# A state-space scan with a squared-ReLU FFN behind it: a new order of work for the first three units, and w_in loaded by halves of contraction

## The chip, the cores and the metric

The kernel runs on one core of a Trainium2 chip. The metric is the device time of one execution in microseconds (us). Engines are called by the profile's names: PE multiplies matrices (PEld is its loading of weights), DVE, ACT and POOL work element by element, SP issues DMAs. PSUM, where PE writes, has eight banks of 128 x 512 float32 values.

## The reference, cut to what matters

Per batch (4) and head (8), a sequence of 768 positions is worked through in chunks of 32 with a carried state; the result goes through an FFN with 3072 tokens, 256 columns and 2048 hidden columns.

```python
cum = np.cumsum(la, axis=-1)
L = np.exp(cum[:, :, :, None] - cum[:, :, None, :]) * causal
CB = np.einsum('bhin,bhjn->bhij', Cc, Bc)
y_intra = np.einsum('bhij,bhjd->bhid', CB * L, xc)
y_inter = np.einsum('bhin,bhnd->bhid', Cc, state) * np.exp(cum)[:, :, :, None]
state = decay_full[:, :, None, None] * state + np.sum(Bx, axis=2)
...
h = np.maximum(x @ w_in, 0.0)
return (h * h @ w_out).astype(np.float32)
```

## The kernel before, in words

The work is cut into 12 units of 256 positions of one batch (all heads), three for each batch. Unit k belongs to the batch k mod 4, so units 0 to 3 are the first ones of the four batches and carry no state in. The products of the decays (P) are made once, for the first 256 positions from `a_nat[0]` and for the rest, later, from `a_nat[1]`.

A unit goes through these steps. Its B and C columns are cast or multiplied with P into the tile `jt` (`pb`, `pc`, lines 158 to 170) and transposed on PE (`tr`, line 195; from unit 4 on by a DMA), and the transposed columns are copied out of PSUM into `bct` (`tc`, line 208 on ACT, 210 on DVE). Its x is multiplied with 1/P into `xs` (`px`, line 177). PE makes the scores in four banks (`mt`, line 220); each bank is masked straight out of PSUM on DVE (`mk`, line 229), or copied by ACT (`sc`, 234) and masked from there on POOL or DVE (`ms`, 238). PE sums the new state (`u`) and the output (`in`, in halves `ina` and `inb`; carried state `ca`; all on line 245). The state for the second half of the unit is made from the sums (`sf`, line 343), ACT copies the sums (`us`), and the output is copied into the FFN's input `T` (`t`; on ACT line 208, on DVE 210).

The FFN has 12 blocks, a to l, one for each unit. A lower case token such as a3 is the fourth of eight pairs of hidden columns of block a: four products of 128x256 with w_in on PE (line 403), then ReLU out of PSUM on ACT into `hb` (line 408); the token qa3 squares it on DVE (414); the upper case token A3 is four products with w_out (line 430). So a pair of columns is about 8 matmuls, and the whole FFN is 784 of the kernel's 1623.

The order is written out by hand in the list `ORDER`: each token issues a step (the table in `one`, lines 655 to 704), and the scheduler leaves the order alone, so each engine works through its own tokens strictly in the order of the list. A token's last letter names the engine: v is DVE, a ACT, p POOL, s SP. Banks are given out in turn by `bank` (line 352).

`id` tokens are idle products of ones with ones (line 476) that write to a free bank and are read by nobody; id3:512 is three of 512 columns. `sp`, `su` make the first P and its totals on PE (lines 452, 521), `ps` and `to` copy them out on ACT; `sk` and `sn` are the scans on DVE, `p2` the second P on PE with two copies on ACT behind it, `fq` and `pq` the small products on POOL that turn the totals into `Pquad`; `iv` is the reciprocal of P on DVE (546). `wm` is a small copy that makes ACT load its table.

Loads go over three queues: SP and ACT (`ld` tokens, line 125), and POOL for the weights, which are cast from float32 to bfloat16 on the way (`wi`, line 139, and `wo`, line 143). POOL issues such a transfer between its other work, in the list's order. w_in is four transfers: number i holds pairs 2i and 2i+1, with both halves of the contraction (2 x 128 rows of w_in). w_out is four transfers of two pairs each.

Of the kernel before, what the change touches and what calls it, by code (L numbers as in the profile page):

```python
# [30 lines left out]
def kernel(  # L31
# [26 lines left out]
        sa3 px4 qc1 pc5 pb5 bk c2 rg4 tr5 C0 mk4 mk4 qc2 c7 qc7 sb0 c3 qc3 d2 d1 C5 za4 afC2 d0 C1 px5 C4 qd2 zb3 C6  # L58
        C3 qd0 d3 C2 mk4 mk4 C7 px6 sa4 rg5 qd3 sb3 pc6 zb4 sb4 pb6 D0 d4 qd1 tr6 mk5 za5 zb5 sa5 sb5 D1 iv:64:96 mk5
        d5 qd4 D2 pb7 d6 qd5 d7 qd6 D3 zb2 e0 qd7 mk5 e1 qe0 sb2 D4 mk5 D5 ld8 pc7 e2 qe1 D6 e3 qe2 px7 D7 rg6 e4 qe3  # L60
        za6 sa6 tr7 zb6 mk6 e5 qe4 sb6 e6 qe5 e7 qe6 mk6 E0 E1 E2 E3 ld9 px8 mk6 f0 qe7 E4 f1 qf0 pc8 E5 pb8 E6 mk6
        f2 qf1 f3 qf2 E7 rg7 mk7 F0 f4 qf3 za7 tr8 F1 F2 f5 qf4 f6 qf5 f7 qf6 g0 qf7 zb7 sa7 sb7 mk7 F3 mk7 F4 pc9
        pb9 px9 ld10 g1 qg0 F5 mk7 g2 qg1 F6 g3 qg2 F7 rg8 za8 zb8 sa8 sb8 g4 qg3 G0 mk8 tr9 g5 qg4 G1 mk8 g6 qg5 G2
        g7 qg6 G3 mk8 h0 qg7 G4 pc10 pb10 px10 ld11 h1 qh0 G5 mk8 h2 qh1 G6 h3 qh2 G7 rg9 za9 zb9 sa9 sb9 h4 qh3 H0
        mk9 tr10 h5 qh4 H1 mk9 h6 qh5 H2 h7 qh6 H3 mk9 i0 qh7 H4 pc11 pb11 px11 i1 qi0 H5 mk9 i2 qi1 H6 i3 qi2 H7
        rg10 za10 zb10 sa10 sb10 i4 qi3 I0 mk10 tr11 i5 qi4 I1 mk10 i6 qi5 I2 i7 qi6 I3 mk10 j0 qi7 I4 j1 qj0 I5 mk10
        j2 qj1 I6 j3 qj2 I7 rg11 za11 zb11 sa11 sb11 j4 qj3 J0 mk11 j5 qj4 J1 mk11 j6 qj5 J2 j7 qj6 J3 mk11 k0 qj7 J4
        k1 qk0 J5 mk11 k2 qk1 J6 k3 qk2 J7 rg12 k4 qk3 K0 k5 qk4 K1 k6 qk5 K2 k7 qk6 K3 l0 qk7 K4 l1 ql0 K5 l2 ql1 K6
        l3 ql2 K7 l4 ql3 L0 l5 ql4 L1 l6 ql5 L2 l7 ql6 L3 ql7"""
    WIN = [(0, 2), (2, 4), (4, 6), (6, 8)]  # L70
    WOUT = [(0, 2), (2, 4), (4, 6), (6, 8)]

# [33 lines left out]
    w_in_b = [wpool.tile([128, 2, (f1 - f0) * 256], BF16, name=f"w_in_b{i}") for i, (f0, f1) in enumerate(WIN)]  # L106
# [29 lines left out]
    def load_w_in(i):  # L136
        f0, f1 = WIN[i]
        n = (f1 - f0) * 256
        nc.gpsimd.dma_start(out=w_in_b[i], in_=_dap(moe_w_in, f0 * 256, [[2048, 128], [128 * 2048, 2], [1, n]]))
# [87 lines left out]

    def ph_mask(k, q):
        nc.vector.tensor_tensor(out=live[k]["mts"][:, q].rearrange("p r g i -> p (r g i)"),  # L229
                                in0=pp[:, q, :], in1=mask, op=ALU.mult)  # L230

    def ph_score(k, q):
        sc = big.tile([128, 512], BF16, tag="sc", name=f"sc{k}_{q}")
        nc.scalar.copy(out=sc, in_=pp[:, q, :])
        live[k].setdefault("sc", {})[q] = sc

    def ph_mask_sb(k, q, eng):
        eng.tensor_tensor(out=live[k]["mts"][:, q].rearrange("p r g i -> p (r g i)"),  # L238
                          in0=live[k]["sc"][q], in1=mask, op=ALU.mult)
# [8 lines left out]
    def ph_carry(k, h, begun):  # L248
# [19 lines left out]
    def ph_intra(k, h, begun, qs=range(4)):  # L268
        v = live[k]
        for g in range(2):  # L270
            for r in range(2):
                for i in range(2):
                    for q in qs:
                        hd = 4 * g + q
                        mm(begun, i, [q], pp[32 * q:32 * q + 32, h[i], g * 128:(g + 1) * 128],
                           v["xs"][64 * i:64 * i + 64, r, hd * 32:hd * 32 + 32],
                           v["mts"][64 * i:64 * i + 64, q, r, g, :], (64 * i, 32 * q))

    def ph_t(k, h, engs=None):
# [71 lines left out]

    def bank():
        h = next(h for h in turn if h not in busy)
# [4 lines left out]
    def pair():  # L358
        free = sorted((turn.index(h), h) for h in turn if h not in busy)
# [36 lines left out]
    def mm1(blk, fp):  # L396

        h = bank()
        gi, o = group_of(WIN, fp)
        w = w_in_b[gi]  # L400
        for i in range(2):
            for g in range(2):
                nc.tensor.matmul(pp[:, h, i * 256:(i + 1) * 256],  # L403
                                 _fap(w, g * w.shape[2] + (o // 2) * 512 + 2 * (o % 2) + i, [[4, 128]]),
                                 T[blk][:, g].rearrange("p r u t -> p (r u t)"),
                                 start=(g == 0), stop=(g == 1), skip_group_check=True)
# [49 lines left out]
    with tc.manual_schedule():  # L456
# [131 lines left out]
        def scores(k):  # L588
# [3 lines left out]
            live[k]["todo"] = [0, 1, 2, 3]  # L592
            live[k]["copied"] = []
            live[k]["masked"] = []

        def mask_direct(k):
            q = live[k]["todo"].pop(0)
            ph_mask(k, q)
            busy.discard(q)
            live[k]["masked"].append(q)  # L600

        def score_copy(k):
            q = live[k]["todo"].pop(0)
            ph_score(k, q)
            busy.discard(q)
# [49 lines left out]
        def one(t):  # L655
            f = t.split(":")
            name = f[0].rstrip("0123456789")
            k = int(f[0][len(name):] or 0)
            if len(name) == 1 and name.lower() in "abcdefghijkl" and len(f[0]) == 2:
                blk = "abcdefghijkl".index(name.lower())  # L660
                if name.islower():
                    mm1(blk, k)
# [5 lines left out]
            if name[0] == "q" and len(name) == 2 and name[1] in "abcdefghijkl":  # L668
# [29 lines left out]
                "u": lambda: first_u(k, f[1] if len(f) > 1 else None), "sf": lambda: ph_sd_first(k),  # L698
                "ca": lambda: ph_carry(k, live[k]["h"], live[k]["begun"]),
# [64 lines left out]
```

## Time and profile before

| | us |
|---|---|
| median of 3 runs | 117.8 (117.77 to 117.89) |
| profiled execution | 116.84 |
| its span, from the first to the last instruction | 115.1 |
| start of the first product with w_in (a0) | 12.20 |
| start of the first product with w_out (A0) | 16.96 |

The profile is of one execution. Times in it are counted from the first instruction. A row of a timeline has the start, the length, the engine, the line, the operation, what is written and read, how many instructions were merged, and in brackets the idle time before them with what ended it. A line of a group has busy time, the mean of one in ns, and idle time before it. L430 is line 430 of the kernel before.

### The profile page before, as it was taken

The page shows a single profiled execution, that of the slowest core. Times are in us where ns is not written, and L with a number is a line of the kernel's source. Part 1 is how long each engine was busy: PE and PEld are TensorE (multiplying, and loading weights), DVE is VectorE, ACT ScalarE, POOL GpSimd, SP SyncE. Part 2 cuts the span into 40 slices and gives each one's busy share as a digit, 9 for nine tenths or more (in the row PEclk, how much of TensorE's full clock was granted, in tenths as well). Part 3 has the DMA queues.
Part 4 walks back from the last instruction along what each step waited for, and adds up shares of the span by engine and source line. Part 5 has one row for each costly group of instructions (what it writes and reads, how often), then busy time and mean ns, then how long its engine had stood idle before and what let it go on. Part 6 is the DMA issues. An engine that isn't in the chain of part 4 may idle for free.

```text
span 115.1 us, 3998 instructions
## 1 busy us (share of the span) xinstructions
PE 108.9 (95%) x1623; PEld 93.5 (81%) x1623; DVE 84.2 (73%) x187; ACT 76.7 (67%) x161; POOL 49.8 (43%) x102
## 2 busy tenths in 40 slices
PE   7977969999999999999999999999999999999990
PEld 2344749978898989989989989989989899899980
DVE  2469996779599969969965989849668488445530
ACT  0655667865598756787486686786777776876840
POOL 7369972068599457548602669038020020000000
PEclk9999999999999999999999999999999999999999
DMA  1999999989999913935915926623023020020202
GB/s 29 199 196 145 199 203 189 215 167 210 180 191 211 214 24 108 160 89 155 179 46 122 178 97 123 132 95 73 0 100 68 0 100 0 6 91 0 91 0 91
DMA packets 47814, 13.46 MB, mean 117 GB/s; under 512 B 44276, under 2 KB 45876, under 8 KB 47796
## 3 DMA queue, kind: packets, MB, share of 16 engines
q1 hardware_dynamic: 43828, 10.64, 44.8%
q0 software_dynamic: 1664, 2.10, 10.8%
q10 hardware_dynamic: 2304, 0.48, 2.0%
q8 instruction: 12, 0.20, 0.8%
q14 instruction: 6, 0.05, 0.1%
HBM read 10.58 MB, written 3.15 MB: 119 GB/s over the span
## 4 chain that ended last, share of the span: by engine, by line
PE 87%; DMA 6%; POOL 2%; issue 1%; DVE 1%; ACT 1%; ACTq 0%; DVEq 0%
PE pp L430 36%; PE pp L403 36%; PE pp L245 6%; DMA w_out_b<-in_moe_w_out_dram 6%; PE pp L476 4%; PE pp L220 3%; POOL mts L238 1%; PE pp L195 1%; POOL jt L158 1%; PE pp L452 1%; DVE jt L158 0%; DVE Sd L343 0%; ACT bct L208 0%; PE pp L521 0%; ACT osl L722 0%
## 5 line engine op out<-in xcount | busy, mean ns | idle before, releaser
L408 ACT ACTIVATE hb<-pp 128x512 bf16<-128x512 f32 x96 | 55.0, 599 | 24.7 <-PE pp L403 23.1
L430 PE MATMUL pp<-w_out_b,h 128*128 128x256 bf16 (+1 forms) x400 | 54.3, 268 | 0.8 <-DMA w_out_b<-in_moe_w_out_dram 0.8
L414 DVE TENSOR_TENSOR h<-hb 128x512 bf16<-128x512 bf16 x96 | 45.0, 486 | 12.7 <-ACT hb L408 12.3
L403 PE MATMUL pp<-T,w_in_b 128*128 128x256 bf16 x384 | 54.2, 273 | 0.0
L403 PEld LDWEIGHTS <-w_in_b 128*128 128x128 bf16 x384 | 41.4, 114 | 2.2 <-issue 1.0
L430 PEld LDWEIGHTS <-h 128*128 128x128 bf16 x400 | 37.6, 98 | 5.4 <-DVE T L210 1.1
L229 DVE TENSOR_TENSOR mts<-pp,mask 128x512 bf16<-128x512 f32 x45 | 29.6, 677 | 3.3 <-PE pp L220 3.3
L331 POOL TENSOR_TENSOR Sd<-z,Pquad 128x256 bf16<-128x256 f32 x16 | 11.1, 693 | 32.9 <-DVE z L315 25.7
L177 POOL TENSOR_TENSOR xs<-x_nat,Pinv 128x256 bf16<-128x256 f32 (+1 forms) x19 | 14.4, 776 | 5.2 <-DVE Pinv L546 4.6
L158 POOL TENSOR_TENSOR jt<-C_nat,P_sb 128x128 bf16<-128x128 f32 x22 | 9.4, 449 | 1.5 <-ACT P_sb L688 1.0
L476 PE MATMUL pp<-const-bfloat16-1.0 128*128 128x512 bf16 (+2 forms) x19 | 7.3, 516 | 0.8 <-PEq L748 0.8
L315 DVE SCALAR_TENSOR_TENSOR z<-z,Ptot,us 128x64 f32<-128x64 f32 x8 | 2.2, 281 | 6.3 <-ACT us L299 5.4
L437 ACT COPY osb<-pp 128x512 f32<-128x512 f32 x11 | 6.3, 584 | 0.4 <-PE pp L430 0.4
L245 PE MATMUL pp<-mts,xs 64*32 64x128 bf16 x384 | 5.9, 219 | 0.1
L170 POOL CAST jt<-B_nat 128x128 bf16<-128x128 f32 x17 | 5.4, 341 | 1.4 <-DMA B_nat<-in_B_dram 1.4
L220 PE MATMUL pp<-bct 32*64 32x256 bf16 x192 | 5.1, 279 | 0.9 <-DVE bct L210 0.6
L476 PEld LDWEIGHTS <-const-bfloat16-1.0 128*128 128x128 bf16 x19 | 2.2, 122 | 4.0 <-issue 3.7
L245 PEld LDWEIGHTS <-xs 64*32 64x32 bf16 x384 | 4.2, 90 | 0.6 <-issue 0.4
L282 ACT CAST T<-pp 128x512 bf16<-128x512 f32 x7 | 4.1, 592 | 0.4 <-PE pp L245 0.2
L208 ACT CAST T<-pp 128x256 bf16<-128x256 f32 x8 | 2.6, 375 | 2.6 <-PE pp L245 2.6
L245 PE MATMUL pp<-bct,Sd 128*128 128x128 bf16 x40 | 4.2, 220 | 0.0
L220 PEld LDWEIGHTS <-bct 32*64 32x64 bf16 x192 | 2.1, 102 | 2.0 <-issue 0.6
(62 smaller groups left out, 53.4 us busy)
## 6 DMA issues: line engine op xcount, KB each, us to landing
x_nat<-in_x_dram SPq DMA_DIRECT2D x11, 256.0 KB, 3.7
out_dram<-osb SPq DMA_DIRECT2D x11, 256.0 KB, 3.2
B_nat<-in_B_dram SPq DMA_DIRECT2D x11, 128.0 KB, 3.1
C_nat<-in_C_dram SPq DMA_DIRECT2D x11, 128.0 KB, 3.4
w_in_b<-in_moe_w_in_dram POOLq DMA_DIRECT2D x4, 256.0 KB, 6.8
w_out_b<-in_moe_w_out_dram POOLq DMA_DIRECT2D x4, 256.0 KB, 8.2
x_nat<-in_x_dram ACTq DMA_DIRECT2D x2, 128.0 KB, 3.4
bct<-jt SPq DMA_TRANSPOSE x8, 3.6
```

Source lines behind the costliest of these rows:

```text
L158: eng.tensor_tensor(out=_fap(jt[k % 3], 128 + 144 * g, [[384, 2], [32, 4], [1, 16]]), in0=_fap(loaded[k]["C"], 128 * g, [[16, 2], [32, 4], ...
L177: eng.tensor_tensor(out=_fap(xs, 256 * r, [[256, 2 // n], [32, 8], [1, 32]]), in0=_fap(loaded[k]["x"], 32 * r, [[32, 2 // n], [64, 8], [1, ...
L220: nc.tensor.matmul(pp[64 * u:64 * u + 64, q, r * 256:r * 256 + 256], bct[32 * q:32 * q + 32, r, 0, u * 64:u * 64 + 64], _fap(bct[32 * q:32 ...
L229: nc.vector.tensor_tensor(out=live[k]["mts"][:, q].rearrange("p r g i -> p (r g i)"), in0=pp[:, q, :], in1=mask, op=ALU.mult)
L245: nc.tensor.matmul(dst, w, v, start=bool(need), stop=False, skip_group_check=True, **({} if pos is None else {"tile_position": pos}))
L331: nc.gpsimd.tensor_tensor(out=_fap(S_d, 0, [[128, 2], [32, 4], [1, 32]]), in0=_fap(z, 0, [[32, 2], [0, 4], [1, 32]]), in1=_fap(Pquad, 4 * ...
L403: nc.tensor.matmul(pp[:, h, i * 256:(i + 1) * 256], _fap(w, g * w.shape[2] + (o // 2) * 512 + 2 * (o % 2) + i, [[4, 128]]), T[blk][:, g].r ...
L408: nc.scalar.activation(out=hb.rearrange("p i t -> p (i t)"), in_=pp[:, h, :], func=AF.Relu)
L414: nc.vector.tensor_tensor(out=h2, in0=hb, in1=hb, op=ALU.mult)
L430: nc.tensor.matmul(dst, h2[:, i, r * 128:(r + 1) * 128], w_out_b[gi][:, 2 * o + i, c0:c1], start=first, stop=(fp == 7 and i == 1), skip_gr ...
L437: nc.scalar.copy(out=osb, in_=pp[:, 6 if blk == 1 else 7, :])
L476: nc.tensor.matmul(pp[:, h, 0:int(cols)], ones_b[:, 0:128], ones_b[:, 0:int(cols)] if dep is None else dep, start=True, stop=True, skip_gr ...
```

## The change

The list `ORDER` is new up to the third unit; from `rg4` on it is as before. `WIN` has two groups of four pairs, and the four transfers of w_in are by pair group and half of contraction: transfers 0 and 1 are the two halves for pairs 0 to 3, transfers 2 and 3 for pairs 4 to 7. The destination of each is 1024 adjacent columns instead of two runs of 512. A token such as a3:0 issues only the two products of a unit that read the first half, a3:1 the other two; in between the bank stays taken. `sf` can be made on ACT, in four activations, one for each quarter. There are 24 idle products instead of 19. Further functions (masks by halves, T by halves, banks named in the list) are added and not used: `HALF` is empty, and the list has no `tg` and no `@`.

```diff
-        id3:512 fa1:a la fa0:s ku ef ldx0:h:a eb id2:512 ti id1:512 gB3 pi ldB0:l:a hd ldC0:l:a ldB0:h:s ldC0:h:s
-        ldx0:l:a wm jz0:v mb jz1:v ldB1:s id3:512 sk pbh0:a id2:512 pk pbl0:p wi0 sp pc0:v ldC1:s trB0 wi1 su iv1:0:8
-        trC0 tcC0:0:v tcB0:2:a id1:512 tcC0:1:a ps pb1:a to px0:v jz2:v mt0 id1:512 u0:67 ldx1:s pc1:p fq sc0 mk0
-        id1:512 mk0 ms0:p tr1 tc1:1:v sc0 tc1:0:a sf0 mt1 ldB2:s wo0 ldC2:s ms0:v ldx2:s id1:384 in0 ca0 iv:8:16
-        id3:512 px1:p t0:aa id1:256 mk1 a0 a1 mk1 mk1 mk1 u1 ina1 inb1 sn1 us0 sf1 qa0 a3 ldC3:s wi2 fr p2 wi3 ca1
-        qa1 wo1 pc2 pb2:a t1:vv us1 iv:32:64 a2 zb0 qa2 zb1 A0 ldB3:s wo2 ldx3:s b3 qb3 b0 pq b2 b1 tr2 wo3 sb1 qa3
-        qb0 A1 b5 b4 qb1 qb2 qb5 tc2:1:v qb4 tc2:0:a a5 B0 b6 B1 a7 qa5 iv:16:32 px2 a6 mt2 B3 A2 sc2 u2 b7 us2 pb3:a
-        pc3 mk2 qa6 px3 mk2 A5 ms2:v mk2 ld4 qb6 sf2 a4 qa7 B5 pc4 A6 A3 ld5 pb4 ina2 inb2 tr4 ca2 t2:aa tr3 B4 B2
-        tc3:0:a tc3:1:a u3:45 qb7 ld6 ld7 mt3 qa4 B6 mk3 mk3 mk3 mk3 us3 c4 c5 c0 A4 A7 B7 c6 qc0 za3 qc4 c1 qc5 qc6
+        id3:512 id1:384 ef pi ti id2:512 id2:512 ku la fa1:a eb id2:512 jz0:v jz2:v fa0:s jz1:p ldx0:h:a ldB0:l:a
+        ldB0:h:s mb wm ldC0:l:a ldC0:h:s ldB1:s sk ldx0:l:a hd wi0 sp id3:512 ldC1:s ps iv:8:16 id2:512 pbh0:p
+        iv1:0:8 pc0:v pbl0:p pk trB0 su tcB0:2:a trC0 ldx1:s tcC0:0:a tcC0:1:v px0:v to id1:512 mt0 id1:128 id2:512
+        mk0 wi1 id1:384 pb1:a u0:67 pc1:p sc0 wi2 tr1 fq id1:128 id1:512 sc0 ms0:p sf0:a wo0 tc1:0:a mk0 tc1:1:v
+        ms0:v ldB2:s mt1 px1:p in0 ca0 id1:256 mk1 ldC2:s t0:aa a1 a0 fr mk1 mk1 ldB3:s u1 ldx2:s us0 mk1 ina1 sf1
+        us1 a2 inb1 ca1 wi3 iv:16:32 ldC3:s a3:0 t1:aa qa1 qa0 id1:512 a3:1 b3 wo1 zb1 sn1 b1 b0:0 ldx3:s p2 pq b0:1
+        wo2 qa3 qb1 iv:32:64 A0 pc2 a5 b4 a6 b6 qb0 qa2 b2 b5 pb2:p qa5 tr2 A1 qb4 sb1 qb3 qa6 tc2:0:a A2 a7 qb2
+        px2:v wo3 B0 pc3 B2 B3 qb5 tc2:1:a mt2 ld4 u2 B1 A5 sf2 qa7 sc2 mk2 B5 mk2 pb3:a ms2:v sc2 ca2 a4 A6 b7 ms2:v
+        tr3 px3:p ina2 inb2 pc4:v us2 tc3:1:v qa4 A3 tc3:0:v qb6 B4 t2:aa mt3 mk3 u3:45 pb4:p qb7 B6 mk3 px4:p ld5
+        tr4 us3 mk3 mk3 c4 qc4 c5 c0 pc5:v ld6 A4 pb5:v c6 qc0 B7 A7 za3 sa3 c1 bk zb0 ld7 qc5 c2 qc1 qc6 rg4 tr5 C0
...
-    WIN = [(0, 2), (2, 4), (4, 6), (6, 8)]
+    WIN = [(0, 4), (4, 8)]
...
-    w_in_b = [wpool.tile([128, 2, (f1 - f0) * 256], BF16, name=f"w_in_b{i}") for i, (f0, f1) in enumerate(WIN)]
+    w_in_b = [wpool.tile([128, 1024], BF16, name=f"w_in_b{i}") for i in range(4)]
...
     def load_w_in(i):
-        f0, f1 = WIN[i]
-        n = (f1 - f0) * 256
-        nc.gpsimd.dma_start(out=w_in_b[i], in_=_dap(moe_w_in, f0 * 256, [[2048, 128], [128 * 2048, 2], [1, n]]))
+        h, g = i // 2, i % 2
+        nc.gpsimd.dma_start(out=w_in_b[i], in_=_dap(moe_w_in, h * 1024 + g * 128 * 2048, [[2048, 128], [1, 1024]]))
...
+        if eng is nc.scalar:
+            for q in range(4):
+                nc.scalar.activation(out=_fap(S_d, 32 * q, [[128, 2], [1, 32]]),
+                                     in_=_fap(pp, v["h"][0] * 512 + 256, [[32, 2], [1, 32]]),
+                                     func=AF.Copy, scale=Pquad[:, total(0, b, 0), q:q + 1])
...
-    def mm1(blk, fp):
+    def mm1(blk, fp, part=None):
 
-        h = bank()
+        h = opened.pop((blk, fp)) if part == 1 else bank()
...
-            for g in range(2):
+            for g in (0, 1) if part is None else (part,):
                 nc.tensor.matmul(pp[:, h, i * 256:(i + 1) * 256],
-                                 _fap(w, g * w.shape[2] + (o // 2) * 512 + 2 * (o % 2) + i, [[4, 128]]),
+                                 _fap(w_in_b[2 * gi + g], (o // 2) * 512 + 2 * (o % 2) + i, [[4, 128]]),
```

More of the change, by code (lines that the diff above doesn't have):

```diff
@@ L59 @@
[L59 to L63, printed above, removed]
@@ L350 @@
     busy = set()
+    forced = []
     def bank():
-        h = next(h for h in turn if h not in busy)
+        h = forced.pop(0) if forced else next(h for h in turn if h not in busy)
+        assert h not in busy
         turn.remove(h)
@@ L358, in pair @@
     def pair():
+        if forced:
+            return tuple(bank() for _ in range(2))
         free = sorted((turn.index(h), h) for h in turn if h not in busy)
@@ L591, in scores, with read_out @@
             busy.update(range(4))
-            live[k]["todo"] = [0, 1, 2, 3]
+            live[k]["todo"] = [(g, p) for g in range(2) for p in range(2)] if k in HALF else [0, 1, 2, 3]
             live[k]["copied"] = []
             live[k]["masked"] = []
+        def read_out(k, q):
+            if k not in HALF:
+                busy.discard(q)
+            elif q[0]:
+                busy.difference_update((2 * q[1], 2 * q[1] + 1))
         def mask_direct(k):
@@ L622, in intra @@
             v = live[k]
+            if k in HALF:
+                gs = {"": (0, 1), "a": (0,), "b": (1,)}[part]
+                assert all((g, p) in v["masked"] for g in gs for p in range(2))
+                ph_intra(k, v["h"], v["begun"], range(4), gs)
+                return
             qs = v["masked"][{"": slice(0, 4), "a": slice(0, 2), "b": slice(2, 4)}[part]]
@@ L655, in one @@
         def one(t):
+            t, _, at = t.partition("@")
+            forced[:] = [int(c) for c in at]
             f = t.split(":")
```

81 lines of the change are left out of this document (60 added, 21 removed).

## The prediction

> **What bounds the kernel now.** I read the page's busy line first, then the table by stretches, then the chain of waits, then the timelines of PE, ACT and POOL.
>
> ```profile
> span 115.1 us, 3998 instructions
> PE 108.9 (95%) x1623; PEld 93.5 (81%) x1623; DVE 84.2 (73%) x187; ACT 76.7 (67%) x161; POOL 49.8 (43%) x102
> ```
> ```profile
> 12.20:16.96 4.76, 3.68 (x78) 2.77 (x77) 4.69 (x12) 2.81 (x10) 4.28 (x9) 1.00 1.18 201
> 16.96:30.33 13.37, 13.26 (x206) 11.38 (x207) 9.85 (x24) 9.88 (x24) 5.30 (x9) 1.00 1.10 194
> 30.33:35.77 5.44, 5.44 (x114) 4.88 (x107) 5.11 (x9) 4.25 (x10) 5.30 (x11) 1.00 1.12 187
> 35.77:115.10 79.33, 76.41 (x1120) 69.75 (x1112) 57.11 (x124) 54.24 (x105) 26.56 (x51) 1.00 0.39 90
> ```
> PE bounds the kernel: 95% of the span. In the stretches (columns: length, then busy time of PE, PEld, DVE, ACT, POOL, granted clock, DMA share, GB/s) it is whole from 30.33 on; what 35.77 to 115.10 lacks is the last stores. The two order lists are equal from the token `rg4` on, and PE's first unit behind it (C0) starts at 35.77 in the trace of before. So the change is worth what it does to the moment at which PE reaches C0; after that the same PE work follows, in the same order.
>
> ```profile
> 0.85 4.85 PE L476 MATMUL pp<-const-bfloat16-1.0 128*128 128x512 bf16 x11 [0.85 <-PEq L748]
> 5.63 0.64 PE L452 MATMUL pp<-eye_f,cp 64*64 64x32 f32 x8
> 7.24 0.40 PE L195 MATMUL pp<-eye_b,jt 128*128 128x128 bf16 x4
> 8.09 0.42 PE L220 MATMUL pp<-bct 32*64 32x256 bf16 x16 [0.24 <-ACT bct L208]
> 10.31 0.42 PE L220 MATMUL pp<-bct 32*64 32x256 bf16 x16 [0.64 <-DVE bct L210]
> 10.94 0.45 PE L245 MATMUL pp<-mts,xs 64*32 64x128 bf16 x32
> 11.44 0.93 PE L476 MATMUL pp<-const-bfloat16-1.0 128*128 128x512 bf16 x4
> 12.20 1.03 PE L403 MATMUL pp<-T,w_in_b 128*128 128x256 bf16 x8
> 16.96 0.60 PE L430 MATMUL pp<-w_out_b,h 128*128 128x256 bf16 x4 [0.81 <-DMA w_out_b<-in_moe_w_out_dram]
> 17.39 1.91 PE L403 MATMUL pp<-T,w_in_b 128*128 128x256 bf16 x16
> 30.78 1.47 PE L403 MATMUL pp<-T,w_in_b 128*128 128x256 bf16 x12
> 32.09 1.47 PE L430 MATMUL pp<-w_out_b,h 128*128 128x256 bf16 x12
> ```
> ```profile
> 10.33 6.49 DMA w_out_b<-in_moe_w_out_dram
> ```
> Twelve FFN products start every 1.31 us (30.78 to 32.09), 0.109 each; a unit (four, a lower or upper case token) is 0.44. The FFN starts at 12.20. From there to 16.96 PE is idle for 4.76 - 3.68 = 1.08. A product is drawn 0.27 long while the next starts after 0.11, so at each of four stops 0.16 more is lost: some 1.7 in all. The chain says why it ends at 16.96: A0, the first product with w_out, stands ahead of everything else, and w_out_b0 is on its way for 6.49, from 10.33 to 16.82. From 16.96 to 30.33 only 0.11 of idle and three or four such ends: some 0.55. That is the stock: **2.3 us**, if the FFN did not start later.
>
> **Part 1, from the scan to the first FFN product.** Eleven idle products take 4.85, so 0.43 each; the four at 11.44 run at 0.22 (three of 512 columns and one of 256 in 0.76). In the new list nine and a 384 stand ahead of the token sp: 9 x 0.43 + 0.32, they end at 5.0. sp waits for the scan anyway; I put it at 5.5 (5.63 before). New behind it: five idle products ahead of the B transposes, from about 6.1. Cold they are 2.1 long, at full speed 1.1; the trace is cold at 5.5 and fast at 7.24, and I take one cold and four fast: they end at 7.35. They are partly cover, since DVE now makes two reciprocals ahead of the two C products:
>
> ```profile
> 6.31 0.49 DVE L158 TENSOR_TENSOR jt<-C_nat,pp 128x128 bf16<-128x128 f32 x2 [0.96 <-PE pp L452]
> 7.34 0.26 DVE L546 RECIPROCAL Pinv<-pp 128x16 f32<-128x16 f32 x1 [0.54 <-PE pp L521]
> 3.56 1.28 ACT L487 ACT_TABLE_LOAD   x1 [3.56 <-issue]
> C_nat<-in_C_dram ACTq DMA_DIRECT2D x1, 64.0 KB, 3.2
> ```
> The first (`iv:8:16`) waits for ACT's copy of P (`ps`), which moved ahead of the C products. sp's end at 6.3, the copy 0.2, two reciprocals and two products: the C columns are done at about 7.5 instead of 6.8, and trC0, behind five idle products and su, runs at 7.75 instead of 7.24, the scores of unit 0 (mt0) at 8.5 instead of 8.09. **Loads:** the token `wm` now makes ACT load its table (1.28) ahead of the low halves of C0 and x0; SP's queue keeps its order up to C2, then B3 stands ahead of x2 and C3. C0 is issued at about 3.85 and lands 3.2 later, at 7.0, just when DVE is there; x0 goes 0.5 behind it and is needed at 8.4. I cost both at nothing; each us more would go straight onto the FFN's start.
>
> ```profile
> 5.67 0.30 ACT L512 ACTIVATE pick_p<-pick,cp 64x8 f32<-64x8 f32 x1
> 8.56 1.07 ACT L234 CAST sc<-pp 128x512 bf16<-128x512 f32 x2
> 9.55 0.48 ACT L208 COPY bct<-pp 128x384 bf16<-128x384 bf16 x1
> 11.43 0.65 ACT L208 CAST T<-pp 128x256 bf16<-128x256 f32 x2 [1.41 <-PE pp L245]
> 12.84 1.09 ACT L408 ACTIVATE hb<-pp 128x512 bf16<-128x512 f32 x2 [0.76 <-PE pp L403]
> 15.53 0.17 ACT L538 COPY Ptot<-pp 128x16 f32<-128x16 f32 x1 [0.46 <-PE pp L537]
> 15.59 0.27 ACT L539 COPY P_sb<-pp 128x128 f32<-128x128 f32 x1
> ```
> `sf0:a` makes unit 0's state on ACT in four activations where DVE made one. No row has that shape: below, 0.06 each (Ptot to P_sb, start to start), above, 0.30 (pick_p); I take 0.15, nearer to the copies out of PSUM, so 0.6 (0.24 to 1.2). They stand ahead of tc1:0, the copy (0.48) that unit 1's scores (mt1) wait for; in before it was free on ACT at 9.55. New: two score copies from 8.97 to 10.05, four activations to 10.6, the copy to 11.05, mt1 at 11.1 instead of 10.31. Less of the 384 idle product goes between mt1 and unit 0's sums, so those are at 11.46 instead of 10.94. From there to a0 it was 1.26 (to 12.20), bound by T's two copies; so the first FFN product is at **12.65, 0.45 later** (0.1 to 1.0 by the bounds). The idle products among these are hidden by the same ACT chain.
>
> **Part 2, w_in.** Two transfers by halves of contraction now hold four pairs of columns for both halves, so a0 to a3 and b0 to b3 need w_in_b0 and 1, the rest 2 and 3.
>
> ```profile
> 5.61 1.64 POOL L139 DMA_DIRECT2D w_in_b<-in_moe_w_in_dram  x2 [0.17 <-issue]
> DMA to landing us min/median/max: 5.5/6.8/7.6
> DMA to landing us min/median/max: 6.5/8.2/8.3
> ```
> The landing rows are of w_in, then of w_out. POOL issues the first at about 4.0 (5.61 before) and the second at 5.8, so both are in by 11.3 to 12.3, or 13.4 at the worst: hidden ahead of 12.65, up to 0.75 if not. The third goes at about 8, w_out_b0 at 10.7, w_in_b3 at 12.3. So w_out_b0 lands at 17.2.
>
> **Part 3, from 12.65 to A0.** PE has a1, a0, u1, a2, unit 1's sums, carry and a3 (cut in two, with a 0.22 idle product between) up to 15.4. T1's copies are ACT's now (DVE's before), behind three hb copies of 0.6: done at 15.75, a wait of 0.4. Then b3, b1, b0 and p2: A0 at **17.75**. That is after w_out_b0, so the old wait is gone. Before, A0 was at 16.96 with four units of 0.44 behind it; now seven: 3 x 0.44 - 0.79 = **0.52 ahead**. With the 0.55 of stops behind 16.96, which have to be earned again, up to 1.07.
>
> **Part 4, what is late next: w_out_b2 and 3.**
>
> ```profile
> 14.22 0.78 POOL L158 TENSOR_TENSOR jt<-C_nat,P_sb 128x128 bf16<-128x128 f32 x2
> 15.78 0.40 POOL L542 TENSOR_TENSOR Pquad<-Ptot,quad 128x64 f32<-128x64 f32 x1 [0.24 <-ACT Ptot L538]
> 16.14 0.59 POOL L143 DMA_DIRECT2D w_out_b<-in_moe_w_out_dram  x1
> 18.30 0.61 POOL L331 TENSOR_TENSOR Sd<-z,Pquad 128x256 bf16<-128x256 f32 x1 [1.57 <-DVE z L320]
> 28.12 0.92 POOL L170 CAST jt<-B_nat 128x128 bf16<-128x128 f32 x2
> ```
> On POOL `pq` now stands behind w_out_b1 and ahead of everything of unit 2 and of w_out_b2 and 3. It waits for Ptot, which ACT copies after p2, and p2 has moved behind b0: 17.9 instead of 15.7. POOL stands still from 13.5 to 17.9. Then pq 0.4, w_out_b2 0.6, two products 0.8, two casts 0.9, Sd 0.6: w_out_b3 is issued at 21.3 instead of 16.14. tr2 waits for the casts at 20.7; PE is there at 20.8: no cost, but no cover either. A5, which needs w_out_b2 (18.35 + 6.5 = 24.9), comes at 24.7. A6, the first that needs w_out_b3, stands 17 units (7.43) and 1.0 of small products behind A0: 26.2. The landing is 5.5 to 6.5 after the issue, by the fastest w_in and w_out: 26.8 to 27.8, a stall of 0.6 to 1.6. Below that, queues emptier than in any row could make it nothing; I take 0.8. While PE stands, DVE and ACT catch up with unit 2 and 3, so I add only 0.2 for the other stops.
>
> **The sum:** 0.52 + 0.55 - 0.8 - 0.2 = 0.07 gained. The profiled execution took 116.84 (span 115.1) beside a median of 117.8; the difference of 1.0 lies around the span, so 117.73: **117.7 us**, no change that can be measured. A measurement of this kernel tells about 0.2% (0.24 us) from no change.
>
> Two rules beside the trace. The profile's granted clock reads 1.00 in all stretches, the first too, where products took 0.43: the cadence decides. The Trainium skill, "TensorE: Matmul & The Clock Gate", Part 1, says that the clock opens after a busy window of about 3.4 us that runs free of the kernel's start, so that the number of cold products varies by run; the trace agrees with one change, between 5.5 and 7.24; how far it varies no run here shows. By it a late window would make the five new products cold, the third rival.
>
> ```profile
> q0 software_dynamic: 414, 0.67, 105.4%
> q1 hardware_dynamic: 351, 0.04, 15.0%
> ```
> In the window 18.5 to 22 the weights' queue (q0) and SP's (q1) moved 414 and 351 packets: near one for one, though q0's are far larger. The Trainium skill, "DMA: Bandwidth & Descriptors", section "Queues, rings and completion order", says that each DMA engine goes round the queues that have work, a packet each; the counts agree. By it w_out_b3, alone in its queue, would pass SP's backlog in some 2 us (an estimate) and land without a stall at A6: the sum would be 0.8 better, as in the first rival.
>
> **The rivals.** *w_out in time* (faster): without A6's stall the sum is 0.87, 116.9; for it speaks that q0 holds nothing else then, against it that even the first w_in took 5.5. *w_out late* (slower): the place is A6, the price the landing of w_out_b3 less 26.2; it decides from a landing at 27.1 on, where a stall of 0.9 has eaten the lead. At 27.8 (6.5) the sum is 0.73 the other way, 118.5; if A5 and tr2 are late too, by 0.2 and 0.3, 119.0; I give 118.7. A landing after 8.2, the median of w_out, at 29.5, would be a stall of 3.3 and 120.2, the far end. *Late clock* (slower): the four idle products that I took as fast cost 0.21 more each, 0.85 onto mt0 and all behind it: 118.6. Against it: three runs within 0.12. *The change does nothing*: a0 waits for T, not for w_in, and the lead is spent on stops of the same length: 117.8.
>
> **How the numbers follow.** Forecast 117.7, own range 117.2 to 118.2, chance 0.44 (faster 0.17, within 0.2% 0.19, slower 0.08); w_out in time 0.19, faster; w_out late 0.23, slower; late clock 0.10, slower; nothing 0.04, within. Faster 0.36, same 0.23, slower 0.41. The range 116.8 to 119.0 leaves out the quick end of the first rival and the far end of the second.
>
> **What would show it.** The first w_in product (12.65), mt1 (11.1), T1's copies and A0 (17.75) in the timeline of PE; POOL idle before pq, released by ACT's Ptot; a wait of PE for w_out at A6, and when C0 starts against 35.77. Wrong: a first product past 13.2, or one before 12.2; no wait for w_out behind A0; PE idle for T1 over 1 us; C1 or x0 landing late because the larger w_in packets take their place.

## The result, and the profile after

The changed kernel takes **125.25 us** (median of 4 runs, 124.33 to 126.10) beside 117.78 of the kernel before (4 runs): ratio 1.0648, 95% interval 1.0554 to 1.0743. The forecast was 117.7 with a range up to 119.0. The ratios here and below leave out executions that were over 1.5% longer than the fastest of the same kernel, which the medians do not, and the profiles of e4, e8, e9 and e10 are of such executions.

The page of the profiled execution (125.62 us), first the span and the engines, then the row of the granted clock in 40 slices of 3.1 us:

```profile
span 123.9 us, 4001 instructions
...
PE 112.6 (91%) x1626; PEld 95.0 (77%) x1628; DVE 87.7 (71%) x191; ACT 78.4 (63%) x164; POOL 46.6 (38%) x98
...
PEclk9998559999679999999999999999999999999999
```

The span is 8.8 longer, and the clock row, all 9 before, has two dents: at slices 4 to 6 and at 11 and 12. The table by stretches (length, then busy time of PE, PEld, DVE, ACT, POOL, clock, DMA share, GB/s) cuts the time at unit 0's sums (12.55), just behind the starts of the first FFN product (16.31) and of A0 (22.72), around a stop behind B0 (27.64 to 31.10), and just behind the start of C0 (44.54), from which on both lists are equal:

```profile
9.06:12.55 3.49, 0.55 (x3) 0.19 (x3) 0.97 (x2) 0.93 (x2) 3.18 (x6) 0.84 1.06 187
12.55:16.48 3.93, 3.53 (x77) 1.94 (x77) 3.27 (x7) 1.99 (x7) 2.12 (x3) 0.50 1.06 175
16.48:22.94 6.46, 6.03 (x91) 4.55 (x90) 4.15 (x12) 4.57 (x13) 0.00 (x0) 0.86 0.98 182
...
27.64:31.10 3.46, 0.60 (x6) 0.31 (x4) 3.46 (x4) 1.48 (x4) 2.56 (x5) 1.00 1.08 191
31.10:44.59 13.49, 13.49 (x251) 10.59 (x249) 10.53 (x28) 8.39 (x21) 1.33 (x3) 0.87 0.45 81
44.59:123.90 79.31, 76.35 (x1117) 69.69 (x1112) 57.80 (x125) 54.31 (x105) 27.77 (x54) 1.00 0.41 89
```

The starts are rows of PE's timeline:

```profile
16.31 1.87 PE L441 MATMUL pp<-T,w_in_b 128*128 128x256 bf16 x8 [0.25 <-ACT T L210]
...
22.72 0.60 PE L473 MATMUL pp<-w_out_b,h 128*128 128x256 bf16 x4
...
30.88 1.05 PE L473 MATMUL pp<-w_out_b,h 128*128 128x256 bf16 x8 [2.86 <-DVE h L457]
...
44.54 0.61 PE L473 MATMUL pp<-w_out_b,h 128*128 128x256 bf16 x4
```

From C0 to the end it is 79.36 here and 79.33 before: the whole difference was made ahead of C0, which comes at 44.54 instead of 35.77, 8.77 later. Two stretches have next to no PE work, 9.06 to 12.55 and 27.64 to 31.10, and behind each of them PE works at a lower clock (0.50, then 0.87).

**The first stop.** The chain of waits (start, length, what) has it in one row:

```profile
1.23 3.18 DMA x_nat<-in_x_dram
4.41 0.02 issue
4.43 7.06 DMA x_nat<-in_x_dram
...
11.58 0.92 DVE xs L179
12.50 0.04 issue
12.55 0.33 PE pp L263 x10
```

x0's low half is not issued until x0's high half has landed (1.23 + 3.18 = 4.41): the two transfers share a semaphore. Eight semaphores serve these loads in turn; x0's low half was the ninth load to take one, and is the eleventh in the new list (C1, too, goes ahead of it). Then it takes 7.06, where it took 3.3 before (the last number of the row below; KB, us from issue to landing), and unit 0's sums stand at 12.55 instead of 8.77.

```profile
x_nat<-in_x_dram ACTq DMA_DIRECT2D x1, 128.0 KB, 3.3
```

In the meantime POOL, too, waits 2.65 for C1. What held them up is seen by queue (packets, MB, share of the 16 DMA engines' time; q0 carries the weights, q1 SP's loads, q10 ACT's), first in the stretch 6 to 7 us, then in 7 to 8:

```profile
q1 hardware_dynamic: 610, 0.08, 49.1%
q10 hardware_dynamic: 323, 0.08, 36.0%
q0 software_dynamic: 14, 0.03, 28.1%
```
```profile
q0 software_dynamic: 56, 0.11, 78.7%
q10 hardware_dynamic: 90, 0.02, 11.1%
q1 hardware_dynamic: 5, 0.00, 0.8%
```

POOL issued w_in_b0 at 4.21; its packets begin between 6 and 7. One microsecond later 56 packets of weights hold the engines for 78.7% of the time, SP's queue has gone from 610 packets to 5 and ACT's from 323 to 90.

**The second stop.** The waits up to 35 us (total, times, longest) name DVE's squares, and the wait of pq in POOL's queue (it is put down to the square that ended last; Ptot, which pq reads, was copied by ACT at 22.69, behind p2):

```profile
POOL Pquad L585 <- DVE h L457: 8.3, 1, 8.3
...
PE pp L473 <- DVE h L457: 2.9, 1, 2.9
```

The timelines of DVE, then of POOL, in the same microseconds:

```profile
23.57 7.26 DVE L457 TENSOR_TENSOR h<-hb 128x512 bf16<-128x512 bf16 x7
```
```profile
22.95 0.29 POOL L585 TENSOR_TENSOR Pquad<-Ptot,quad 128x64 f32<-128x64 f32 x1 [8.27 <-DVE h L457]
23.19 0.59 POOL L145 DMA_DIRECT2D w_out_b<-in_moe_w_out_dram  x1
23.80 0.99 POOL L160 TENSOR_TENSOR jt<-C_nat,P_sb 128x128 bf16<-128x128 f32 x2
...
27.36 1.04 POOL L179 TENSOR_TENSOR xs<-x_nat,Pinv 128x512 bf16<-128x512 f32 x1
28.35 0.71 POOL L172 CAST jt<-B_nat 128x128 bf16<-128x128 f32 x2
29.03 1.18 POOL L179 TENSOR_TENSOR xs<-x_nat,Pinv 128x256 bf16<-128x256 f32 x2
```

Seven squares take 7.26, over 1 us each on average and up to 1.98, where before three took 1.14. pq comes through at 22.95, and then POOL does in one unbroken run, up to 30.2, what it had spread from 14 to 30 before.

### The profile page after: what moved, and what is told of

Its sections match the earlier page's. It is cut to its first block, busy times and chain, and to the rows that moved or that the text cites. A ratio compares the mean times of both kernels' runs of the same rounds, so it can differ in the third digit from the quotient of the medians.

```text
span 123.9 us, 4001 instructions
## 1 busy us (share of the span) xinstructions
PE 112.6 (91%) x1626; PEld 95.0 (77%) x1628; DVE 87.7 (71%) x191; ACT 78.4 (63%) x164; POOL 46.6 (38%) x98
## 4 chain that ended last, share of the span: by engine, by line
PE 83%; DMA 8%; DVE 3%; ACT 2%; issue 1%; ACTq 0%; DVEq 0%
PE pp L473 36%; PE pp L441 35%; DMA x_nat<-in_x_dram 8%; PE pp L263 7%; PE pp L222 4%; DVE h L457 2%; ACT Sd L370 1%; DVE xs L179 1%; ACT T L210 1%; PE pp L197 1%; DVE Sd L375 0%; ACTq L118 0%; PE pp L495 0%; ACT bct L210 0%; PE pp L580 0%
## 5 line engine op out<-in xcount | busy, mean ns | idle before, releaser
L473 PE MATMUL pp<-w_out_b,h 128*128 128x256 bf16 (+1 forms) x400 | 55.5, 273 | 2.9 <-DVE h L457 2.9
L457 DVE TENSOR_TENSOR h<-hb 128x512 bf16<-128x512 bf16 x96 | 48.8, 526 | 11.1 <-ACT hb L451 11.0
L441 PE MATMUL pp<-T,w_in_b 128*128 128x256 bf16 x384 | 55.1, 276 | 0.3 <-ACT T L210 0.2
L241 DVE TENSOR_TENSOR mts<-pp,mask 128x512 bf16<-128x512 f32 x44 | 29.0, 679 | 2.3 <-PE pp L222 2.3
L179 POOL TENSOR_TENSOR xs<-x_nat,Pinv 128x256 bf16<-128x256 f32 (+1 forms) x18 | 13.3, 759 | 0.1
L160 POOL TENSOR_TENSOR jt<-C_nat,P_sb 128x128 bf16<-128x128 f32 x18 | 8.0, 462 | 2.7 <-DMA C_nat<-in_C_dram 2.7
L519 PE MATMUL pp<-const-bfloat16-1.0 128*128 128x512 bf16 (+3 forms) x22 | 7.7, 479 | 0.9 <-PEq L811 0.8
L263 PE MATMUL pp<-xs,jt 64*32 64x64 bf16 x160 | 3.1, 206 | 2.9 <-DVE xs L179 2.9
L263 PEld LDWEIGHTS <-jt 64*32 64x32 bf16 x160 | 1.7, 92 | 5.1 <-issue 4.3
```

What stands on the lines that cost most here:

```text
L160: eng.tensor_tensor(out=_fap(jt[k % 3], 128 + 144 * g, [[384, 2], [32, 4], [1, 16]]), in0=_fap(loaded[k]["C"], 128 * g, [[16, 2], [32, 4], ...
L179: eng.tensor_tensor(out=_fap(xs, 256 * r, [[256, 2 // n], [32, 8], [1, 32]]), in0=_fap(loaded[k]["x"], 32 * r, [[32, 2 // n], [64, 8], [1, ...
L263: nc.tensor.matmul(dst, w, v, start=bool(need), stop=False, skip_group_check=True, **({} if pos is None else {"tile_position": pos}))
L441: nc.tensor.matmul(pp[:, h, i * 256:(i + 1) * 256], _fap(w_in_b[2 * gi + g], (o // 2) * 512 + 2 * (o % 2) + i, [[4, 128]]), T[blk][:, g].r ...
L457: nc.vector.tensor_tensor(out=h2, in0=hb, in1=hb, op=ALU.mult)
L473: nc.tensor.matmul(dst, h2[:, i, r * 128:(r + 1) * 128], w_out_b[gi][:, 2 * o + i, c0:c1], start=first, stop=(fp == 7 and i == 1), skip_gr ...
```

## The experiments

Each changed kernel was run beside the kernel before on the same chip. "List" is the order list; moves are shown as its fragments.

| run | what it is | us, median | ratio to before, 95% |
|---|---|---|---|
| after | the change | 125.25 | 1.0648 [1.0554, 1.0743] |
| e1 | C0's and x0's low halves ahead of ACT's table load | 123.90 | 1.0546 [1.0482, 1.0610] |
| e2 | pq back behind w_out_b3 | 122.69 | 1.0442 [1.0383, 1.0501] |
| e3 | e1 and e2 | 121.17 | 1.0345 [1.0252, 1.0439] |
| e4 | before's list, new w_in layout | 118.29 | 1.0065 [1.0026, 1.0103] |
| e5 | w_in issued later | 120.34 | 1.0203 [1.0131, 1.0275] |
| e6 | e5 and e2 | 119.31 | 1.0148 [1.0090, 1.0205] |
| e7 | e6, loads ahead as in e1 | 119.74 | 1.0147 [1.0056, 1.0239] |
| e8 | sixteen idle products in the first stop | 126.08 | (122.82 to 127.92, no interval) |
| e9 | e7, two idle products more ahead of sp | 118.95 | 1.0213 [1.0159, 1.0267] |
| e10 | e9 with the old w_in layout | 117.95 | 1.0086 [1.0037, 1.0136] |
| e11 | e10, three idle products fewer | 117.88 | 1.0125 [1.0067, 1.0184] |
| e12 | before, with three POOL products more | 117.77 | 1.0151 [1.0082, 1.0221] |
| e13 | the change with the old w_in layout | 126.13 | 1.0630 [1.0532, 1.0728] |
| e14 | before, with w_in issued earlier | 119.37 | 1.0130 [1.0070, 1.0189] |

**e1, e2, e3: the two stops, by undoing one move each.** e1 is the change with the loads' fragment altered, e2 with pq's, e3 with both.

```diff
- ldx0:h:a ldB0:l:a ldB0:h:s mb wm ldC0:l:a ldC0:h:s ldB1:s sk ldx0:l:a hd wi0 sp
+ ldx0:h:a ldB0:l:a ldC0:l:a ldB0:h:s ldC0:h:s ldx0:l:a mb wm ldB1:s sk hd wi0 sp
```
```diff
- p2 pq b0:1
+ p2 b0:1
...
- px2:v wo3 B0
+ px2:v wo3 pq B0
```

> One part undone: the low halves of C0 and x0 are issued by ACT ahead of its table load, and B1 behind them, as in the kernel before; the rest is the changed kernel. Theory (two separate stalls: x0's low half late behind w_in, and later squares held up by POOL): x0's low half lands by 7.5 instead of 11.49, unit 0's sums (u0) start at 9.1 to 9.8 instead of 12.55, the first product with w_in comes at 12.3 to 13.2 instead of 16.48, the half clock from 11.4 to 18.3 is gone, and the time is 119.5 to 122; the stall at B2 stays. Rival (the larger w_in packets, issued early, starve whatever is loaded beside them, wherever x0 stands): x0 or the next load (C1, x1) is late all the same, u0 or mt1 still waits over 2 us for a load, and the time is 123.5 to 125.5.

> Only the token pq moves: from ahead of w_out_b2 to behind w_out_b3, so POOL no longer stands still from w_out_b1 to the second P. Theory (squares on DVE are held up while POOL works without a pause behind pq): squares between 23 and 31 take about 0.4 instead of up to 2.0, PE's wait of 2.9 at B2 falls under 0.5, the half clock from 31.9 to 35.3 is gone, and the time is 120 to 122.5; the stall at u0 stays. Rival (the squares wait for hb, or DVE for x2 by a load that is late): the squares stay late, PE waits over 2 at B2, and the time is 124 to 125.5.

> Both edits together. Theory (the two stalls and the clock that they cost are the whole loss): 116.5 to 118.3, with the first product with w_in at 12.3 to 13.2 and no half clock before the end. Rival (starved loads): above 120.

e1 fell to the rival: 123.9. Ahead of ACT's table load x0's low half still stood in front of a taken semaphore (now that of the second transfer of a_nat) and was issued at 4.4. It came 2 us sooner all the same, the sums were at 10.37, and POOL then waited 4.2 for C1. e2 was 122.69, 0.2 past what the theory gave. Its timeline of DVE:

```profile
25.08 2.11 DVE L457 TENSOR_TENSOR h<-hb 128x512 bf16<-128x512 bf16 x5
```

The squares are back at 0.42, the stop behind B0 and the second dent of the clock are gone: pq's place is worth about 2% of this kernel as long as the first stop is there. In e3 (rival again: 121.17) the sums come at 10.42, and the timeline of PE shows the next load in line:

```profile
11.83 0.96 PE L197 MATMUL pp<-eye_b,jt 128*128 128x128 bf16 x5 [0.99 <-POOL jt L160]
```

These are unit 1's transposes behind POOL's product with C1. The first stop is no matter of x0 alone; with x0 mended, C1 is late.

**e4: the layout alone.** The list of before in the changed kernel.

> The other way round: the list of the kernel before, with only w_in loaded by halves of contraction in rows of 1024 columns. Theory (the layout by itself does no harm where w_in goes out after x0): 117.2 to 118.4, x0 and C1 landing as before. Rival (larger w_in packets starve the loads): x1, B2 or C2 land more than 2 us later than in the kernel before, and the time is over 119.

118.29, ratio 1.0065: as the theory had it, a small loss, and no stop ahead of unit 0's sums. In the profiled execution (119.74) PE waits 1.36 and 1.28 for the third and fourth transfers of w_in, at 20.9 and 22.5.

**e5, e6, e7: w_in's first transfer later.** e5 is the change with one move; e6 adds e2's, e7 also issues the loads ahead of the table load, with the first transfer of a_nat ahead of the second.

```diff
- hd wi0 sp
+ hd sp
...
- pc0:v pbl0:p pk
+ pc0:v pbl0:p wi0 pk
```

> The changed list with one move: POOL issues w_in_b0 behind its two B0 copies (about 5.6 instead of 4.21); everything else as changed, pq too. Theory (the early w_in transfer starves the small-packet loads x0 low half and C1, which are issued at 4.4 and 4.0): x0's low half lands by 8.5 instead of 11.49, C1 by 9, PE's stall ahead of unit 0's sums falls from 3.5 us to under 1, the half clock at 11.4 goes, and the stall at B2 behind pq stays: 119.5 to 122. Rival (the loads are late because they are themselves issued late, behind their semaphore slots, and any w_in transfer in flight then does the same): x0 low still lands beyond 10, and the time is 123.5 to 125.5.

> As the run before, and pq stands behind w_out_b3 again. Theory (two separate causes that add): both stalls gone, no half clock after 7 us, 116.8 to 118.5. Rival (a third cause is left: C1, with w_in_b1 issued at about 6.1 to 6.6): POOL still waits for C1 over 2 us, mt1 beyond 13, 119 to 121.5.

> As the run before, and the low halves of C0 and x0 are issued ahead of ACT's table load, with the first a transfer ahead of the second as before the change, so that x0's low half meets a free semaphore slot. x0 low is expected issued at about 3.0 and landed by 6.5. Theory (loads decide the start, the new layout and the idle products cost next to nothing): first FFN product at 12.2 to 12.7, 116.5 to 117.8. Rival (the two-kilobyte packets of w_in still slow C1 and x1 enough to delay mt1 by 1 us or more): 118 to 119.5.

e5's theory held for the loads and for the time. w_in_b0 is issued at 5.79. In the stretch 7 to 8 us, where the changed kernel had 5 packets of SP's queue, it has

```profile
q1 hardware_dynamic: 1057, 0.24, 111.6%
q10 hardware_dynamic: 36, 0.01, 3.8%
```

and none of weights. x0's low half, issued at 4.54 behind the same taken semaphore as in the changed kernel, landed 3.7 later, and the timeline of PE runs through, up to the first products with w_in:

```profile
9.63 0.25 PE L263 MATMUL pp<-xs,jt 64*32 64x64 bf16 x16
...
11.37 0.42 PE L222 MATMUL pp<-bct 32*64 32x256 bf16 x16 [0.77 <-ACT bct L210]
...
14.03 0.95 PE L441 MATMUL pp<-T,w_in_b 128*128 128x256 bf16 x7 [0.85 <-DMA w_in_b<-in_moe_w_in_dram]
```

Unit 1's scores (the second row) are at 11.37; the forecast had 11.1. So 1.6 us of issue time on one transfer is worth 4.5% here (1.0648 to 1.0203), with everything else of the change in place. One part of the theory failed: the stop behind B0 should have stayed, since pq stands where it stood, and it shrank from 2.86 to 0.23:

```profile
25.00 1.05 PE L473 MATMUL pp<-w_out_b,h 128*128 128x256 bf16 x8 [0.23 <-DVE h L457]
```

pq comes through at 19.71 here, and POOL's unbroken run ends at 24.3, where it waits for x2. So the two stops are not separate causes: most of the second one came with the early w_in too.

With pq moved too, e6 and e7 stay at 1.015, in or just above the rivals' times, but not for the rivals' reasons: POOL waits only 1.36 and 0.85 for C1, and unit 1's scores are late (13.15 and 13.21) because unit 0's already were (10.30 and 10.35), with the clock at half until 10.08 and 9.66. e7 did not do to the loads what was expected: x0's low half was issued at 4.38 again, not at 3.0, behind the semaphore of the second transfer of a_nat.

**e8: the clock apart from the stop.** The change with `id16:512` ahead of `u0:67`.

> The changed list with 16 idle products of 512 columns more ahead of unit 0's sums, which fill PE's stall from 9.06 to 12.55. It prices the half clock (11.43 to 18.26) apart from the stall that brought it on. Theory (the half clock is a cost of its own): full clock through 18.3, gain 1.5 to 3 us, 122.3 to 123.8. Rival (in that stretch PE waits for C1, x1 and w_out anyway, so its clock does not matter): 124.6 to 125.8.

This settles nothing. Of its four executions the one with a mean granted clock of 1.0 took 122.82, inside the theory's numbers; the profiled one (127.92) ran the first 12.8 us at half clock, so that the scores stood at 10.5 and the sixteen products took 3.8 ahead of work that was ready. What the half clock costs apart from the stop stays open.

**e9, e10, e11: what is left, the idle products and the layout.** In e7's profile the clock was granted later than in e5's. The timeline of PE there, and in e9, which has two idle products more ahead of sp (`hd sp` becomes `hd id2:512 sp`):

```profile
6.35 2.32 PE L519 MATMUL pp<-const-bfloat16-1.0 128*128 128x512 bf16 x5
```
```profile
6.09 1.26 PE L519 MATMUL pp<-const-bfloat16-1.0 128*128 128x512 bf16 x5
```

> The run e7_loads_and_pq with two idle products of 512 columns more between the scan and sp, where PE stood idle from about 4.95 to 5.7 while the clock was still half. Theory (the clock is granted at points 3.41 us apart, for the work PE did before the point; the gap in the idle products made it miss one, so that in that run's profile PE ran at half clock up to 9.66 and unit 0's scores came at 10.35 instead of 8.5): the clock is full by 6.7 in most executions, unit 0's scores at 8.4 to 8.8, time 117.2 to 118.2. Rival (the late clock is chance, whatever the idle products are): scores again beyond 10 in the profiled execution, 118.8 to 120.

> The run e9_no_gap with w_in as before the change: four transfers of two pairs of columns, both halves of contraction, in packets of one kilobyte. Theory (with the halves the first product has to wait for two transfers instead of one): the wait for w_in at the first two FFN products (1.48 in the run that issues w_in later) goes, time 0.6 to 1.2 below e9_no_gap, 116.2 to 117.4. Rival (the layout costs nothing once the loads in front of it are in time): within 0.3 of e9_no_gap.

> The run e10_no_gap_old_layout with two instead of five idle products between sp and unit 0's B transposes. Theory (three more idle products at full clock cost 0.66 at most, and part of it lies beside DVE's two C products): unit 0's scores 0.2 to 0.4 earlier, time 0 to 0.5 below e10. Rival (they keep the clock up): the clock is late in more executions and the median is up by 0.5 or more.

e9's five idle products are fast and its scores stand at 8.58 instead of 10.35, as the theory said, but this does not show that the gap was the reason: the change itself, e1, e2, e3, e5 and e13 have the same gap, and in their profiles the clock is full by 4.4 to 6.0. Chance stays possible. The time is not lower (1.0213 beside 1.0147, intervals that overlap). That a late clock costs the end anything was not shown. e10's theory held in the difference (1.0 us); its time lies above the forecast one. The first FFN products in e9, then in e10:

```profile
12.98 0.27 PE L441 MATMUL pp<-T,w_in_b 128*128 128x256 bf16 x1 [0.41 <-ACT T L210]
14.53 0.97 PE L441 MATMUL pp<-T,w_in_b 128*128 128x256 bf16 x7 [1.28 <-DMA w_in_b<-in_moe_w_in_dram]
```
```profile
12.96 1.03 PE L440 MATMUL pp<-T,w_in_b 128*128 128x256 bf16 x8 [0.41 <-ACT T L209]
```

With halves of contraction the first unit needs two transfers: one product, and then a wait of 1.28 for the second (0.85 in e5). With the old layout eight run in a row. The medians differ by 1.0 us. e11 (`sp id3:512 ldC1:s` becomes `sp ldC1:s`) is not to be told from e10: its scores came 0.23 earlier, as forecast, but three idle products more or less cost nothing that shows in the time. No version beat the kernel before; about 1% (0.4 to 1.4) is left in e10, and its cause was not settled. In e11's profile POOL waits for C2, with w_out_b3 behind it in its queue:

```profile
POOL jt L159 <- DMA C_nat<-in_C_dram: 6.7, 2, 6.5
```

**e12: are the squares late because POOL works beside them?** The kernel before, with three products that nobody needs, behind unit 1's state:

```diff
+ busy_in = _fap(eye_f, 0, [[0, 4], [1, 128]])
+ busy_out = const.tile([128, 4, 128], BF16, name="busy_out")
+ def pool_busy():
+     for _ in range(3):
+         P.tensor_tensor(out=busy_out, in0=busy_in, in1=busy_in, op=ALU.mult)
...
- wo3 sb1 qa3
+ wo3 sb1 pz qa3
```

> The kernel before, and nothing of the change, with three products of 128 x 512 on POOL put behind unit 1's state (about 18.9 to 22.0, where POOL had no work): their inputs and output lie in SBUF and nothing waits for them. Theory (DVE's squares cannot run beside an unbroken row of POOL's products): one or more of the squares between 19 and 22, 0.41 to 0.47 each before, takes 1 us or more, PE waits for squares, time 0.5 to 3 us above before. Rival (the squares were late because pq held up POOL's queue, not because POOL worked beside them): squares stay under 0.7, time 117 to 118.

POOL's row, DVE's and the first row of PE behind it:

```profile
19.10 3.42 POOL L554 TENSOR_TENSOR busy_out<-eye_f 128x512 bf16<-128x512 f32 x3
```
```profile
17.72 5.41 DVE L414 TENSOR_TENSOR h<-hb 128x512 bf16<-128x512 bf16 x5
```
```profile
20.49 0.61 PE L430 MATMUL pp<-w_out_b,h 128*128 128x256 bf16 x4 [0.45 <-DVE h L414]
```

And DVE in the same microseconds of the kernel before:

```profile
18.72 1.14 DVE L414 TENSOR_TENSOR h<-hb 128x512 bf16<-128x512 bf16 x3 [0.57 <-ACT hb L408]
...
20.19 0.76 DVE L414 TENSOR_TENSOR h<-hb 128x512 bf16<-128x512 bf16 x2 [0.32 <-ACT hb L408]
```

Five squares take 5.41 with POOL at work and 1.90 (1.14 + 0.76) without; PE waits 0.45 for one and later 0.73 for a copy that DVE makes behind them, and the time goes up by 1.5%. The time alone lies in both forecasts; the squares decide for the theory. Nothing waits for the added products and they take no place in a queue that something needs, so it is their running beside DVE that costs.

**e13, e14: the earlier issue or the larger packets?** e13 is the change with w_in in the four transfers of before, issued as early as in the change; e14 the kernel before with POOL's first w_in transfer moved.

```diff
- ldx0:l:a wm jz0:v
+ ldx0:l:a wi0 wm jz0:v
...
- pbl0:p wi0 sp
+ pbl0:p sp
```

> The changed list, with w_in in four transfers of two pairs of columns as before (packets of one kilobyte), issued as early as in the changed kernel (about 4.2). Theory (the early issue does it, whatever the packet): x0's low half lands beyond 9.5 and PE stands 2 us or more ahead of unit 0's sums, 122 to 125. Rival (the two-kilobyte packets do it): x0's low half lands by 8.5, no half clock at 11 to 18, 119 to 121.

> The list and the layout of before, with one move: POOL issues w_in_b0 ahead of its wait for B0, at about 3.7 instead of 5.61. x0's low half is issued at 3.0 here, ahead of it; C1 (4.8) and x1 (5.3) come behind it. Theory (an early w_in transfer starves the loads that are issued around or behind it): C1 lands 1 to 3 us later than at 7.8, x1 beyond 12, unit 1's scores 0.5 to 2 us later, 118 to 120.5. Rival (only loads held up by their own semaphore slot are late): C1 by 8.3, and the time is 116 to 117.5, no higher than before or even lower, since w_in is there earlier.

Both theories held in their direction. e13's time, 126.13, is above its range, and PE stands in two places, 1.03 ahead of unit 0's sums (2 or more were forecast) and 1.64 ahead of unit 1's scores. In e13 x0's low half lands 5.5 after its issue (7.06 with the larger packets) and POOL waits 3.9 for C1, so that the scores of unit 1 come at 13.82. In e14 x0 is out of the way (issued at 3.0, in by 6.4), and C1 is what suffers. Its row in the kernel before (KB, us from issue to landing), then in e14:

```profile
C_nat<-in_C_dram SPq DMA_DIRECT2D x1, 128.0 KB, 2.8
```
```profile
C_nat<-in_C_dram SPq DMA_DIRECT2D x1, 128.0 KB, 5.5
```

The scores of unit 1 come at 12.50 instead of 10.31, the clock drops to half from 11.1 to 17.9, and the kernel is 1.3% slower for a transfer that was issued 2.0 us sooner. The packet's size is not needed for it.

## Why the prediction was wrong

**What bounds the kernel** held: the change is worth what it does to the time at which PE reaches C0, and the rest is 79.3 in both.

**Part 1, up to the scores, held**: sp at 5.56 (5.5 forecast), trC0 at 7.55 (7.75), unit 0's scores at 8.42 (8.5). C0's low half was in at 6.2 (7.0). The four activations of `sf0` took 0.93, over the 0.6 taken and inside the bounds (0.24 to 1.2).

**The step that failed** is "I cost both at nothing", said of the loads of C0 and x0. For C0 it was right. x0's low half was put "0.5 behind it"; it was issued 1.3 behind, at 4.43, since the eleventh load to take a semaphore waits for an earlier one, and it landed at 11.49, against a need at 8.4. The text gave the price of such a delay, that each us would go straight onto the FFN's start, and the sign to look for, C1 or x0 landing late because the w_in packets take their place. Neither got a time or a chance. e5 shows that the delay of the issue alone would have cost little: with the same late issue and w_in out of the way it lands 3.7 later, and the sums are at 9.63.

**Part 2 failed with it, in its direction.** The earlier w_in (4.0 forecast, 4.21 measured) was asked only whether it would itself be in time. The first transfer was (6.4 after its issue, at 10.6). The second landed 7.9 after its issue at 6.08, at 13.9, past the 13.4 that the text gave as the worst; it cost nothing here by luck, because the first product came only at 16.31. What the earlier w_in does to the loads in flight was the question, and e14 answers it by itself: 1.3%. The row that should have led there stood in the prediction: 414 packets of weights beside 351 of SP's between 18.5 and 22, one for one although the first are far larger. I used it for w_out_b3 alone. Applied to 4.2 us it says that SP's and ACT's small packets fall to the weights' pace as soon as these arrive, and the changed kernel's 7 to 8 us shows that, or worse.

**Part 3**: the first FFN product at 16.31 (12.65 forecast) and A0 at 22.72 (17.75). The order's own gain, three units ahead, can only be estimated, from a sum. From the first FFN product to C0 it is 28.23 instead of 23.57, 4.66 more. The stop behind B0 gives 2.86 of that (3.46 less 0.60). The lower clock gives about 1.75 (0.13 of 13.49) and 0.90 (0.14 of 6.46) if PE was the limit all that time, which e8 could not settle. Together that is 5.5, so some 0.9 would have been won back, near the forecast lead of up to 1.07; no run shows it by itself. The halves of the layout, costed at nothing or 0.75 at most, cost 1.28 at the first product once the loads are in time (e9).

**Part 4** had the right token and the wrong victim. pq did block POOL (8.27; the forecast was 13.5 to 17.9, 4.4) and did push w_out_b3's issue (25.79, forecast 21.3). No product waited for w_out. "While PE stands, DVE and ACT catch up with unit 2 and 3" is the sentence that failed: the work that POOL had not done came in one run, and e12 shows that DVE's squares are then held up beside it.

**The chances.** The rival that forecast slower named w_out at A6 and ended at 120.2. No case had a stop of 3 us ahead of unit 0's sums, nor one behind DVE, and none had the clock fall again behind a stop; the third rival knew the clock only as late. So the range had no reason to reach 125.

**How much belongs to what**, by the ratios: the early w_in 4.5% of the 6.5% (e5, whose nine executions lie between 118.71 and 122.08), pq 2% with it and not surely anything without (e5 and e6 overlap), the layout 0.65% in the old list (e4), about 1.3% in the new one once w_in is later (e9, e10) and nothing that shows beside the early w_in (e13), three of the idle products nothing that shows (e11), and about 1% unexplained (e10). These shares overlap and do not add up.

## What to carry to other kernels

When a bulk transfer is moved forward, ask what is in flight when its packets arrive (some 2 us behind its issue here), not only whether it is in time itself; small-packet loads that a first stage waits for must have landed by then. When an instruction that waits is moved ahead on a queue, what it holds back comes later in one run: look for who shares something with that engine at that time. And count the loads ahead of a moved load: one more can make it wait for the semaphore of an earlier one.

## What the runs showed of the hardware

**Weights against small loads.** In the changed kernel all queues together moved 947 packets between 6 and 7 us and 151 between 7 and 8, when the weights came (56 of the 151, for 78.7% of the engines' time). The Trainium skill, "DMA: Bandwidth & Descriptors", section "Queues, rings and completion order", has each engine go round the queues that have work, a packet at a time; ACT's 90 packets against 56 agree with it roughly, SP's 5 do not, while SP had C1, x1 and B2 outstanding. The section's packet holds several descriptors; no run here shows whether the profile counts the same unit. In e14, too, SP moved 4 packets beside 112 of the weights, between 6 and 7 us. In the changed kernel SP's issue of C2 then lasted 4.85 us (1.48 before). Why SP's queue stood still was not tried.

**DVE beside POOL.** The Trainium skill, "SBUF — State Buffer", section "SBUF: two separate sides", says that a DVE instruction with two inputs in SBUF and a POOL instruction that reads SBUF exclude each other for a whole instruction. e12 agrees: squares of 0.41 to 0.47 become up to 1.96. Such a square is longer than any one of POOL's products there (1.04 to 1.12), and in the changed kernel one took 1.98 beside four of POOL's instructions: it looks as if DVE did not get its turn between two that follow without a pause.

**The clock.** In all these traces it changes at points 3.41 us apart or a multiple of it (in the changed kernel 4.61, 11.43, 18.26, 31.91, 35.33). It fell to half at 11.43 and at 31.91 although PE had 1.27 and 1.03 us of work in the 3.41 before these points, and it came back 6.83 and 3.41 later. The amount of work alone does not decide: in e1 it fell at 12.70 after 1.91 us of work, and stayed full at 29.77 after 1.43.
